# A root of the norm by bits, one Newton step and a third-order step, on rows that one product with ones brings to all partitions

## The chip, the cores and the metric

One core of one Trainium2 chip runs the whole program. The metric is the device time of one execution in microseconds (us). A span, as the trace gives it, is some 2 us shorter than the time. The words TensorE, VectorE, ScalarE, GpSimd stand for the engines that the profile calls PE (PEld for its weight loads), DVE, ACT, POOL.

## The reference

```python
# attention: batch 8, heads 8, sequence 576, head size 64 (retention with decay)
x = attention_output          # 4608 tokens x 512
rms = np.sqrt(np.mean(x * x, axis=-1, keepdims=True) + 1e-06)
xn = x / rms * rms_g
g = xn @ w_gate               # 512 x 1536
silu = g * (1.0 / (1.0 + np.exp(-g)))
val = xn @ w_val
return (silu * val @ w_out).astype(np.float32)
```

Everything is fp32. The tokens are worked in 12 units of 384. Channels lie on partitions (4 blocks of 128), tokens along the free axis. So the mean of squares is a sum over partitions, and its root is wanted on every partition, because each channel of a token is multiplied by the same number.

## The kernel before

The norm of unit u+1 is worked while TensorE does the last product of unit u, a down projection in seven products of 12 matmuls (xo, zo, wo, yo, xo, zo, wo).

```python
def norm_1(u):                       # mean of squares, one column per 128 tokens
    ms = bank(f"ms_{u}")
    for s in range(NS):              # NS = 3
        nc.tensor.matmul(ms[:, s : s + 1], lhsT=t_of[u][:, s * P : s * P + P], rhs=mean_w, ...)
    r = tmp.tile([P, NS], F32, ...)
    nc.vector.tensor_scalar(out=r, in0=ms[:, :NS], scalar1=EPS, scalar2=None, op0=ALU.add)
    nc.gpsimd.tensor_tensor(out=r, in0=r, in1=mhalf.to_broadcast([P, NS]), op=ALU.pow)
    t_of[u] = r

def diagonals(u):                    # three diagonal matrices of the roots
    for s in range(NS):
        nc.vector.tensor_scalar(out=t_of[u][:, s * P : s * P + P], in0=ident,
                                scalar1=r[:, s : s + 1], scalar2=None, op0=ALU.mult)

def norm_2(u):                       # ones times diagonal: the roots as rows on all partitions
    rb = bank(f"rb_{u}")
    nc.tensor.matmul(rb[:, :U], lhsT=ones, rhs=t_of[u], start=True, stop=True)
    for c in range(NHP):             # NHP = 4
        nc.vector.scalar_tensor_tensor(out=x[:, c], in0=x[:, c], scalar=rms_g[:, c : c + 1],
                                       in1=rb[:, :U], op0=ALU.mult, op1=ALU.mult)
    # ... four differences of blocks of x, for the seven-product form of the up projection

# in the loop over units, between the products of across(u):
    # behind xo, zo, wo: norm_1(u + 1), diagonals(u + 1)
    # behind yo, xo:     norm_2(u + 1)
```

`norm_0` before this squares x on ScalarE and adds the four blocks up on VectorE.

Of the kernel before, what the change touches and what calls it, by code (L numbers as in the profile page):

```python
# [10 lines left out]
F32 = mybir.dt.float32  # L11
U32 = mybir.dt.uint32
AF = mybir.ActivationFunctionType
ALU = mybir.AluOpType
P = 128
# [26 lines left out]
def kernel(  # L42
# [11 lines left out]
    nc = tc.nc  # L54
    B, H, S, D = q.shape
    NTOK, DM = out.shape
    DFF = moe_w_gate.shape[1]
    NHP = H // 2
# [5 lines left out]
    U = 384  # L64
    HU = U // 2
    NS = U // P
    NU = NTOK // U
    NH = NF // 2
    NG = NH // 2
    EPS = 1e-6  # L70
    assert (D, DM, NHP * P) == (64, H * D, DM) and S % SQ == 0 and NTOK % U == 0
    assert NC * L == S and NC == 2 * NFULL + 1 and TAIL == L == D and NHP == 4 and NH % 2 == 0
    assert (2 * S) % U == 0 and B % 2 == 0 and S == 3 * HU

    const = ctx.enter_context(tc.tile_pool(name="const", bufs=1))
# [11 lines left out]
    def bank(name):  # L87
        return banks.tile([P, 512], F32, tag="b", name=name)

    def temp(name):  # L90
        return tmp.tile([P, U], F32, tag="t", name=name)

    def cell(name, value):
        t = const.tile([P, 1], F32, name=name)
        nc.vector.memset(t, value)
        return t

    ones = const.tile([P, P], F32, name="ones")
# [10 lines left out]
    gc = const.tile([P, NHP], F32, name="gc")  # L109
    tick = const.tile([1, 1], F32, name="tick")  # L110
    rms_g = const.tile([P, NHP], F32, name="rms_g")
    w_out = const.tile([P, NF, DM], F32, name="w_out")


# [14 lines left out]
    x_of, t_of, h_of, first_places = {}, {}, {}, {}  # L129
# [3 lines left out]
    def load_qk(j):  # L133
        b, hp = jobs[j]
        for nm, src in (("q", q), ("k", k)):

            t = raw.tile([P, S // SQ, SQ], F32, tag=nm + "raw", name=f"{nm}raw_{j}")
            for e in range(2):
                rows = src[b, 2 * hp + e].rearrange("(t b) (i a) -> i b t a", b=SQ, a=SQ)
                for i in range(D // SQ):  # L140
                    r = e * D + i * SQ
                    nc.sync.dma_start(out=t[r : r + SQ], in_=rows[i])
            st[j][nm + "raw"] = t
# [56 lines left out]
    def load_kv(j):  # L200

        b, hp = jobs[j]
        for nm, src, bufs in (("k", k, 4), ("v", v, 3)):
            t = raw.tile([P, NFULL, 2, D], F32, tag=nm, name=f"{nm}_{j}", bufs=bufs)
            for e in range(2):
                nc.sync.dma_start(
                    out=t[:, :, e],
                    in_=src[b, 2 * hp + e, : NFULL * P].rearrange("(c p) d -> p c d", p=P),
                )
            st[j][nm] = t  # L210
        t = st[j]["vt"] = raw.tile([L, 2, D], F32, tag="vt", name=f"vt_{j}", bufs=3)
        nc.sync.dma_start(
            out=t, in_=v[b, 2 * hp : 2 * hp + 2, NFULL * P :].rearrange("e p d -> p e d")
        )
# [182 lines left out]
    def slot(j, rest=True):  # L397

        if j > len(jobs):
            return  # L400
        if rest and j > 0:
            values(j - 1)
        if j < len(jobs):
            scores(j)
            states(j)
        if j < len(jobs):
            weigh(j)
        if j < 2 * NHP:
            sums(j)
        if rest and j > 0:  # L410
            carried(j - 1)
        if 2 * NHP <= j < len(jobs):
            sums(j)

    def prepare_next(j):
        if j + 1 < len(jobs):
            prepare(j + 1)

    def load_next(j):
        if j + 2 < len(jobs):  # L420
            load_qk(j + 2)
            load_kv(j + 2)
# [11 lines left out]

    def gather(u, c, sq):

        if c:
            nc.vector.tensor_tensor(out=t_of[u], in0=t_of[u], in1=sq, op=ALU.add)
        else:
            t_of[u] = sq  # L440

    def norm_0(u):
        for c in range(NHP):
            gather(u, c, square(u, c))

    def norm_1(u):
# [7 lines left out]
        r = tmp.tile([P, NS], F32, tag="r", name=f"r_{u}", bufs=1)  # L454
        nc.vector.tensor_scalar(out=r, in0=ms[:, :NS], scalar1=EPS, scalar2=None, op0=ALU.add)
        nc.gpsimd.tensor_tensor(out=r, in0=r, in1=mhalf.to_broadcast([P, NS]), op=ALU.pow)
        t_of[u] = r

    def diagonals(u):
        r = t_of[u]  # L460
        t_of[u] = temp(f"diag_{u}")
        for s in range(NS):
            nc.vector.tensor_scalar(
                out=t_of[u][:, s * P : s * P + P], in0=ident, scalar1=r[:, s : s + 1],
                scalar2=None, op0=ALU.mult,
            )

    def norm_2(u):



        x = x_of[u]
        rb = bank(f"rb_{u}")
        nc.tensor.matmul(rb[:, :U], lhsT=ones, rhs=t_of[u], start=True, stop=True)
        for c in range(NHP):
            nc.vector.scalar_tensor_tensor(  # L476
                out=x[:, c], in0=x[:, c], scalar=rms_g[:, c : c + 1], in1=rb[:, :U],
                op0=ALU.mult, op1=ALU.mult,
            )
        if u < 2:  # L480
            return
        b11, b12 = x[:, :2, :HU], x[:, :2, HU:]
        b21, b22 = x[:, 2:, :HU], x[:, 2:, HU:]
        t = ffn.tile([P, 3, 2, HU], F32, tag="sums", name=f"sums_{u}")
        t2, t3, t4 = (t[:, i] for i in range(3))
        for o, a, b in ((t3, b22, b12), (b12, b12, b11), (t2, b22, b12), (t4, b21, t2)):
            nc.vector.tensor_tensor(out=o, in0=a, in1=b, op=ALU.subtract)

        t_of[u] = b11, b21, b12, t4, t2, t3, b22
# [116 lines left out]
    def fetch():  # L606
        nonlocal n_fetched
        if n_fetched < 7 * (NU - 2):
            nc.sync.dma_start(
                out=w_slots[:, n_fetched % 4], in_=w_blocks[ORDER[n_fetched % 7]]  # L610
            )
            n_fetched += 1
# [233 lines left out]
    def start():  # L846
# [32 lines left out]
        for j in range(2 * NHP):  # L879
            slot(j)  # L880
            if j + 1 < 2 * NHP:
                turn(j + 1)
            if squares:
                gather(*squares.pop())
            for i in ((1,), (2,), (3,), (4, 5), (6,), (7,), (), ())[j]:
                scale_v(i)
            if j:
                u, c = divmod(j - 1, NHP)
                squares.append((u, c, square(u, c)))
            act(1)  # L890
            if j == 5:
                norm_1(0)
            elif j == 6:
                norm_2(0)
            weights((2, 0, 0, 1, 1, 1, 1, 0)[j])
            if j == 4:
                gather(*squares.pop())
            elif j == 5:
                diagonals(0)
            act(1)  # L900
# [33 lines left out]
        for i, _ in enumerate(rest):  # L934
            if i == 1:
                norm_0(2)
            elif i == 3:
                norm_1(2)
                diagonals(2)
# [5 lines left out]
        for i, _ in enumerate(rest):  # L945
            if i == 2:
                norm_2(2)
# [10 lines left out]
    def behind(u, i):  # L958
        at, n = SLOTS[u % 3]
        if i in at:  # L960
            j = u // 3 * 8 + n + at.index(i)
            slot(j)
            turns.append(j)
            if i < 2 * NG - 1:
                load_next(j)
        if u + 1 < NU and i >= 5:
            (norm_0, norm_1, norm_2)[i - 5](u + 1)
            if i == 6:
                diagonals(u + 1)

    with tc.manual_schedule():
        start()
        for u in range(2, NU):
            for i in range(2 * NG):
                for n, _ in enumerate(up(u, i % 2, i // 2)):
                    if n == 2 and turns:
                        prepare_next(turns.pop())
                if i in (1, 3):
                    fetch()
                    fetch()  # L980
                if i == 2 * NG - 1:
                    rest = across(u)
                    next(rest)
                behind(u, i)
            for i, _ in enumerate(rest):
                if i == 0 and turns:
                    prepare_next(turns.pop())
                if i == 2:
                    behind(u, 6)
                    at, n = SLOTS[u % 3]  # L990
                    if 2 * NG - 1 in at:
                        load_next(u // 3 * 8 + n + len(at) - 1)
                elif i == 4:
                    behind(u, 7)

# [26 lines left out]
```

## Time and profile before

| | before |
|---|---|
| time, median of the first three runs | 1151.86 us |
| time, median with three more runs | 1151.6 us |
| span of the trace (its run took 1153.15 us) | 1151.4 us |
| TensorE / weight loads busy | 98% / 91% |
| VectorE / ScalarE / GpSimd busy | 62% / 21% / 4% |

A row of the timeline reads: start and duration in us, engine, line of the kernel, operation, output<-inputs, and how many instructions were merged. The bracket gives the idle time of the engine before it and what ended that idle time. TensorE executes each fp32 matmul as two instructions, so a product of 12 matmuls shows as x24. The duration of a TensorE row is modelled, so costs are taken from one start to the next. The prediction below shows the rows themselves: TensorE has no idle time around the norm, VectorE has several holes.

### The profile page before, as it was taken

How to read it: one execution, taken by the hardware profiler on the slowest of the kernel's cores; microseconds unless marked ns; L12 is line 12 of the kernel's file. 1: busy time of each engine (PE TensorE's matmuls, PEld its weight loads, DVE VectorE, ACT ScalarE, POOL GpSimd, SP SyncE). 2: the span in 40 equal slices, each digit the busy share in tenths (PEclk: the TensorE clock that was granted, in tenths of full speed). 3: DMA queues.
4: the chain of work that ended last, by engine and by line, in shares of the span. 5: the costliest groups of instructions: out<-in, count | busy, mean ns of one | idle time of the engine just before them, and what ended most of it. 6: DMA issues, size and time to landing. Idle time of an engine off the chain costs nothing.

```text
span 1151.4 us, 24802 instructions
## 1 busy us (share of the span) xinstructions
PE 1126.5 (98%) x10524; PEld 1053.4 (91%) x10524; DVE 716.0 (62%) x1420; ACT 244.0 (21%) x480; POOL 50.8 (4%) x74
## 2 busy tenths in 40 slices
PE   8799999989999999999999999999999999999998
PEld 6655557989999999999999999999999999999998
DVE  5788858675675675365766675465576566445352
ACT  5546542002201211211221120120220220120210
POOL 0000000570000000000000000000000000000000
PEclk8999999999999999999999999999999999999999
DMA  8764336335453565044345456306436503403304
GB/s 203 207 184 147 109 131 193 56 59 117 115 130 67 146 141 160 1 105 102 97 119 73 116 144 119 114 29 120 117 80 140 144 19 93 128 1 99 122 1 110
DMA packets 292943, 125.42 MB, mean 109 GB/s; under 512 B 270432, under 2 KB 275808, under 8 KB 292832
## 3 DMA queue, kind: packets, MB, share of 16 engines
q1 hardware_dynamic: 282688, 107.66, 38.1%
q10 hardware_dynamic: 10144, 16.16, 4.3%
q8 instruction: 83, 1.36, 0.5%
q14 instruction: 28, 0.23, 0.1%
HBM read 108.83 MB, written 14.94 MB: 108 GB/s over the span
## 4 chain that ended last, share of the span: by engine, by line
PE 90%; DVE 3%; DMA 2%; POOL 1%; ACT 1%; issue 1%; SPq 0%; DVEq 0%; POOLq 0%; ACTq 0%
PE x L507 14%; PE w L507 14%; PE z L507 13%; PE up L564 8%; PE xo L629 8%; PE wo L629 7%; PE zo L629 7%; PE y L507 7%; PE yo L629 4%; PE av L351 2%; PE av L370 2%; PE s L280 2%; POOL w_gate L811 1%; PE s L300 1%; DMA w_gate<-in_moe_w_out_dram 1%
## 5 line engine op out<-in xcount | busy, mean ns | idle before, releaser
L531 ACT COPY m<-x 128x384 f32<-128x384 f32 x60 | 28.8, 479 | 449.8 <-PE x L507 425.5
L629 PE MATMUL xo<-h,w_out 128*128 128x192 f32 x528 | 90.3, 328 | 0.0
L507 PE MATMUL w<-sums,w_val 128*128 128x192 f32 x480 | 88.6, 328 | 0.6 <-DVE c L514 0.3
L507 PE MATMUL x<-x,w_gate 128*128 128x192 f32 x480 | 89.0, 329 | 0.0
L507 PE MATMUL x<-x,w_val 128*128 128x192 f32 x480 | 88.8, 328 | 0.0
L507 PE MATMUL z<-x,w_gate 128*128 128x192 f32 x480 | 87.8, 326 | 0.0
L507 PE MATMUL w<-sums,w_gate 128*128 128x192 f32 x480 | 87.8, 326 | 0.0
L507 PE MATMUL z<-x,w_val 128*128 128x192 f32 x480 | 87.8, 326 | 0.0
L629 PEld LDWEIGHTS xo<-h,w_out 128*128 128x128 f32 x528 | 85.9, 190 | 0.6
L629 PE MATMUL wo<-h,w_out 128*128 128x192 f32 x504 | 85.3, 326 | 0.0
L629 PEld LDWEIGHTS wo<-h,w_out 128*128 128x128 f32 x504 | 82.5, 190 | 0.0
L514 DVE TENSOR_TENSOR u<-m,y 128x384 f32<-128x384 f32 x60 | 33.1, 552 | 79.2 <-PE y L507 79.1
L507 PEld LDWEIGHTS w<-sums,w_val 128*128 128x128 f32 x480 | 79.2, 190 | 2.9 <-DVE c L514 2.9
L507 PEld LDWEIGHTS x<-x,w_gate 128*128 128x128 f32 x480 | 79.6, 191 | 0.5
L507 PEld LDWEIGHTS z<-x,w_gate 128*128 128x128 f32 x480 | 79.8, 190 | 0.0
L507 PEld LDWEIGHTS x<-x,w_val 128*128 128x128 f32 x480 | 79.1, 190 | 0.6
L507 PEld LDWEIGHTS z<-x,w_val 128*128 128x128 f32 x480 | 79.6, 190 | 0.0
L507 PEld LDWEIGHTS w<-sums,w_gate 128*128 128x128 f32 x480 | 79.6, 190 | 0.0
L514 DVE TENSOR_TENSOR h<-u,w 128x384 f32<-128x384 f32 x60 | 33.0, 551 | 71.0 <-PE w L507 71.0
L526 ACT ACTIVATE h<-h 128x384 f32<-128x384 f32 x90 | 47.1, 523 | 88.6 <-DVE h L514 88.6
L564 PE MATMUL up<-x,w_gate 128*128 128x384 f32 x192 | 63.3, 488 | 0.9 <-DVE x L476 0.7
L564 PE MATMUL up<-x,w_val 128*128 128x384 f32 x192 | 62.7, 487 | 0.2 <-ACT w_val L572 0.2
(170 smaller groups left out, 1769.8 us busy)
## 6 DMA issues: line engine op xcount, KB each, us to landing
w_out<-w_blocks SPq DMA_DIRECT2D x70, 768.0 KB, 5.1
out_dram<-o SPq DMA_DIRECT2D x368, 24.0 KB, 1.6
qraw<-in_q_dram SPq DMA_DIRECT2D x96, 72.0 KB, 2.7
kraw<-in_k_dram SPq DMA_DIRECT2D x96, 72.0 KB, 2.8
k<-in_k_dram SPq DMA_DIRECT2D x48, 128.0 KB, 3.0
v<-in_v_dram SPq DMA_DIRECT2D x48, 128.0 KB, 2.9
w_out<-in_moe_w_gate_dram ACTq DMA_DIRECT2D x5, 1024.0 KB, 5.8
w_out<-in_moe_w_out_dram ACTq DMA_DIRECT2D x3, 1024.0 KB, 4.9
```

Source lines behind the costliest of these rows:

```text
L280: nc.tensor.matmul(s[side(odd), e, i * L : i * L + L], lhsT=d["kT"][side(e), c * L : c * L + L], rhs=d["qT"][side(e), c * L : c * L + L], ...
L300: nc.tensor.matmul(o[side(e)], lhsT=d["k"][side(odd), i, e], rhs=d["v"][side(odd), i, e], start=True, stop=True,)
L351: mm = nc.tensor.matmul(av[odd][column(j, odd, e), i * L : i * L + L], lhsT=d["v"][side(odd), i, e] if c < NC - 1 else d["vt"][:, e], rhs= ...
L370: mm = nc.tensor.matmul(av[odd][column(j, odd, e), i * L : i * L + L], lhsT=d["sum"][side(e), c - 1], rhs=d["qT"][side(e), c * L : c * L + L],
L507: nc.tensor.matmul(ps[:, i * HU : i * HU + HU], lhsT=w_up[m][:, 2 * blk + c, cut], rhs=t_of[u][blk][:, c], start=(start and i == c == 0), ...
L514: nc.vector.tensor_tensor(out=o, in0=a, in1=pairs_of(ps), op=ALU.add)
L526: nc.scalar.activation(out=o, in_=c, func=AF.Silu)
L531: nc.scalar.copy(out=s1, in_=pairs_of(x_))
L564: nc.tensor.matmul(ps[:, :U], lhsT=w_up[m][:, 4 * half + c, i * P : i * P + P], rhs=x_of[u][:, c], start=(c == 0), stop=(c == NHP - 1),)
L629: nc.tensor.matmul(ps[:, i * HU : i * HU + HU], lhsT=a[:, c, i * P : i * P + P], rhs=rhs[:, c], start=(start and i == c == 0), stop=False, ...
L811: nc.gpsimd.tensor_tensor(out=o, in0=a, in1=b, op=op)
```

## The change

The intent: leave the detour by columns. The squares are summed over partitions by one product with ones, whose result stands on all partitions as rows at once. The inverse root is then computed on 128x384 elements: a first guess out of the bits of the number, one Newton step and one third-order step. This is done for units 3 to 11; the first three keep the old way. (In parts of the diff that are not printed here, EPS moves into the last addition of the squares, and constants are folded into the weights of the norm.)

```diff
+    rms_k = const.tile([P, NHP], F32, name="rms_k")
+    guess = cell("guess", 0x5F1FFFF9 + 2.0**22 * np.log2(DM))
...
+    def root_1(u):
+        y = t_of[u]
+        s = bank(f"ms_{u}")[:, :U]
+        nc.tensor.matmul(s, lhsT=ones, rhs=y, start=True, stop=True)
+        e = temp(f"e_{u}")
+        nc.scalar.activation(
+            out=y.bitcast(U32), in_=s.bitcast(U32), func=AF.Relu, bias=guess, scale=-0.5
+        )
+        nc.scalar.activation(out=e, in_=y, func=AF.Square)
+        nc.vector.scalar_tensor_tensor(
+            out=e, in0=e, scalar=-1.0 / DM, in1=s, op0=ALU.mult, op1=ALU.mult
+        )
+        nc.vector.scalar_tensor_tensor(
+            out=y, in0=e, scalar=K0, in1=y, op0=ALU.add, op1=ALU.mult
+        )
+        nc.scalar.activation(out=e, in_=y, func=AF.Square)
+        t_of[u] = y, e, s
+
+    def root_2(u):
+        y, e, s = t_of[u]
+        nc.vector.scalar_tensor_tensor(
+            out=e, in0=e, scalar=K1 * K1 / DM, in1=s, op0=ALU.mult, op1=ALU.mult
+        )
+        nc.vector.scalar_tensor_tensor(
+            out=e, in0=e, scalar=-10.0 / 3.0, in1=e, op0=ALU.add, op1=ALU.mult
+        )
+        nc.vector.scalar_tensor_tensor(
+            out=s, in0=e, scalar=5.0, in1=y, op0=ALU.add, op1=ALU.mult
+        )
+        t_of[u] = s
...
     def norm_2(u):
-        rb = bank(f"rb_{u}")
-        nc.tensor.matmul(rb[:, :U], lhsT=ones, rhs=t_of[u], start=True, stop=True)
+        g = rms_k
+        rb = t_of[u]
+        if u < 3:
+            g = rms_g
+            rb = bank(f"rb_{u}")[:, :U]
+            nc.tensor.matmul(rb, lhsT=ones, rhs=t_of[u], start=True, stop=True)
...
-            (norm_0, norm_1, norm_2)[i - 5](u + 1)
-            if i == 6:
-                diagonals(u + 1)
+            (norm_0, root_1, norm_2)[i - 5](u + 1)
...
+                elif i == 3 and u + 1 < NU:
+                    root_2(u + 1)
```

More of the change, by code (lines that the diff above doesn't have):

```diff
@@ L70 @@
     EPS = 1e-6
+    K0, K1 = 2.38924456, 0.703952253
     assert (D, DM, NHP * P) == (64, H * D, DM) and S % SQ == 0 and NTOK % U == 0
@@ L435, in gather @@
     def gather(u, c, sq):
-        if c:
+        if c == NHP - 1 and u > 2:
+            nc.vector.scalar_tensor_tensor(
+                out=t_of[u], in0=t_of[u], scalar=EPS * DM / P, in1=sq, op0=ALU.add, op1=ALU.add
+            )
+        elif c:
             nc.vector.tensor_tensor(out=t_of[u], in0=t_of[u], in1=sq, op=ALU.add)
@@ L457, in norm_1 @@
         t_of[u] = r
+    def root_1(u):
[23 more added lines that the diff above has]
+        )
+        nc.vector.scalar_tensor_tensor(
+            out=s, in0=e, scalar=5.0, in1=y, op0=ALU.add, op1=ALU.mult
+        )
+        t_of[u] = s
     def diagonals(u):
@@ L472, in norm_2 @@
         x = x_of[u]
-        rb = bank(f"rb_{u}")
-        nc.tensor.matmul(rb[:, :U], lhsT=ones, rhs=t_of[u], start=True, stop=True)
+        g = rms_k
[4 more added lines that the diff above has]
+            nc.tensor.matmul(rb, lhsT=ones, rhs=t_of[u], start=True, stop=True)
         for c in range(NHP):
             nc.vector.scalar_tensor_tensor(
-                out=x[:, c], in0=x[:, c], scalar=rms_g[:, c : c + 1], in1=rb[:, :U],
+                out=x[:, c], in0=x[:, c], scalar=g[:, c : c + 1], in1=rb,
                 op0=ALU.mult, op1=ALU.mult,
@@ L966, in behind @@
         if u + 1 < NU and i >= 5:
-            (norm_0, norm_1, norm_2)[i - 5](u + 1)
-            if i == 6:
-                diagonals(u + 1)
+            (norm_0, root_1, norm_2)[i - 5](u + 1)
     with tc.manual_schedule():
         start()
+        nc.vector.tensor_scalar(
+            out=rms_k, in0=rms_g, scalar1=3.0 / 8.0 * K1, scalar2=None, op0=ALU.mult
+        )
         for u in range(2, NU):
```

## The prediction

> **What bounds the kernel now.** I read the engine table of the page first, then the chain that ended last, then the list of what TensorE waited for, and last the timeline of one place where the changed lines run.
>
> ```profile
> PE 1126.5 (98%) x10524; PEld 1053.4 (91%) x10524; DVE 716.0 (62%) x1420; ACT 244.0 (21%) x480; POOL 50.8 (4%) x74
> PE 90%; DVE 3%; DMA 2%; POOL 1%; ACT 1%; issue 1%; SPq 0%; DVEq 0%; POOLq 0%; ACTq 0%
> ```
>
> TensorE is busy for 98% of the span and weight loads for 91%; VectorE for 62%, ScalarE 21%, GpSimd 4%. The chain that ended last is TensorE for 90%. The table by stretches says more: from 300 us on, every full 100 us holds 99.65 to 100.00 us of TensorE work, at a granted clock of 1.00. The non-TensorE parts of the chain lie before 250 us, in the start. So in the steady part time can be gained only by taking work out of TensorE's stream, and lost only if something makes TensorE wait.
>
> The norm of each 384-token unit u+1 is worked in the shadow of unit u's last product (the seven-product form of the down projection: products xo, zo, wo, yo, xo, zo, wo). The timeline around 330 us shows the norm of the fourth unit, the first that changes:
>
> ```profile
> 326.07 4.06 PE L629 MATMUL wo<-h,w_out 128*128 128x192 f32 x24
> 326.61 1.35 DVE L641 TENSOR_TENSOR h<-h 128x1152 f32<-128x1152 f32 x1
> 327.88 0.77 DVE L251 STREAM_TRANSPOSE qT<-qraw 128x576 f32<-128x576 f32 x1
> 328.57 0.73 DVE L251 STREAM_TRANSPOSE kT<-kraw 128x576 f32<-128x576 f32 x1
> ...
> 329.97 0.72 PE L450 MATMUL ms<-mean_w,sq 128*128 128x1 f32 x6
> ...
> 330.55 4.15 PE L629 MATMUL yo<-h,w_out 128*128 128x192 f32 x24
> 330.73 0.16 DVE L455 TENSOR_SCALAR r<-ms 128x3 f32<-128x3 f32 x1 [1.43 <-PE ms L450]
> 330.97 0.86 POOL L456 TENSOR_TENSOR r<-r,mhalf 128x3 f32<-128x3 f32 x1 [14.04 <-DVE r L455]
> 331.87 0.68 DVE L463 TENSOR_SCALAR diag<-ident,r 128x128 f32<-128x128 f32 x3 [0.98 <-POOL r L456]
> ...
> 334.54 4.06 PE L629 MATMUL xo<-h,w_out 128*128 128x192 f32 x24
> 334.81 0.56 DVE L638 TENSOR_TENSOR u2o<-m1o,yo 128x384 f32<-128x384 f32 x1 [2.26 <-PE yo L629]
> ...
> 338.44 0.81 PE L474 MATMUL rb<-diag,ones 128*128 128x384 f32 x2
> 338.64 0.58 DVE L651 STREAM_TRANSPOSE o<-xo 128x384 f32<-128x384 f32 x1 [1.49 <-PE xo L629]
> ...
> 339.08 4.06 PE L629 MATMUL zo<-h,w_out 128*128 128x192 f32 x24
> 339.14 1.32 DVE L641 TENSOR_TENSOR h<-h 128x1152 f32<-128x1152 f32 x1
> 340.38 2.18 DVE L476 SCALAR_TENSOR_TENSOR x<-x,rms_g,rb 128x384 f32<-128x384 f32 x4
> ```
>
> The reader is to see three things. The TensorE rows follow each other without an idle bracket, so ms and rb are paid in full. VectorE, in contrast, has holes: 1.43 us before r, 0.98 us before diag, 2.26 us before u2o, 1.49 us before the xo transpose. And GpSimd's power works on 128x3 elements in 0.86 us that nobody on TensorE waits for. The next such places (424, 510, 601 us and so on) repeat these figures within some hundredths.
>
> **What the Trainium skill says.** "TensorE: Matmul & The Clock Gate", section LDWEIGHTS, gives a weight load as columns / 1.2 ns, 107 ns for 128 columns. The six one-column ms matmuls therefore should be bound by their six loads; the trace shows 0.72 us for six, 120 ns each, so it agrees roughly. "VectorE: DVE Perf Modes", section The TRN2 errata, gives (N+151)/0.96 ns for an fp32 tensor_tensor, 557 ns for N=384; the trace has 551 to 558. "ScalarE: Activation LUTs", section What ACT_TABLE_LOAD costs, gives 186 + 0.833 N ns with immediates, 506 ns for 384, and about 93 ns more for a [128,1] bias; the trace's Square has 522. Its section Table sets says cheap functions such as relu are in every set. The trace agrees so far: there is one table load in all, though Silu, Square, Copy and Relu all run, so the new Relu should bring no load.
>
> **The change part by part**, for the nine norms of units 3 to 11 (places at 330, 424, 510, 601, 695, 781, 871, 964 and 1047 us).
>
> TensorE. From wo's first matmul (326.07) to xo's (334.54) are 8.47 us. A 24-matmul product alone takes 342.98 - 339.08 = 3.90 us (the next wo starts at 342.98 in the same timeline), so ms costs 8.47 - 7.80 = 0.67 us. In the same way rb costs 339.08 - 334.54 - 3.90 = 0.64 us. The change puts one product with ones on 384 columns at the place of ms: the shape of rb, so 0.64 us; and it drops rb. Net per norm: 0.64 - 0.67 - 0.64 = -0.67 us. Nine norms: -6.0 us. In instructions: each norm loses six ms and two rb matmuls and gains two, so TensorE should have 10524 - 54 = 10470.
>
> VectorE. Removed per norm: r 0.16 and three diag at 0.283, 1.0 us. Added: five scalar_tensor_tensor on 128x384; the existing one of that size takes 0.606, so 3.0 us; and the last gather becomes one too (0.61 for 0.555). Sum +2.1 us a norm, +19 us over nine: 716 becomes about 735, 64%. ScalarE gains three activations, the first with a pointer bias from PSUM: about 1.6 us a norm, +15 us. GpSimd loses nine powers at about 0.85, -7.7 us. All of this lies beside TensorE's stream, if it fits the holes.
>
> Does it fit? The order of the built program answers where each piece stands. Two scalar_tensor_tensor replace r and diag before u2o, and three stand between the first output transpose and the xo transpose. First part: the ones product ends near 330.6. Relu, Square, two VectorE steps and a Square form one dependent chain: 0.55 + 0.52 + 0.61 + 0.61 + 0.52 = 2.8 us, and some 0.1 to 0.2 us per handover (r started 0.18 us after yo, behind ms). The VectorE steps end near 333.4, ahead of u2o at 334.8; the last Square ends near 334.1. Second part: the first output transpose ends at 337.15. Three dependent steps at about 0.63 take 1.9 us, to 339.0. The xo transpose then starts some 0.4 us later than its 338.64, and so do h (L641) and the four x multiplies. Against this, TensorE now runs 0.67 us earlier. The deadlines: the last wo product needs h (L641), ready near 340.9, and starts at 342.3, slack 1.4 us. The next unit's first product needs two of the x multiplies, ready near 341.9, and starts at 346.2. Its second needs the sums, ready near 344.7, and starts at 347.5. Nothing becomes a wait of TensorE.
>
> **The rivals.** (1) VectorE takes the place of the wait: the three extra steps push h past the last wo product. For it: this is the tightest deadline, 2.5 us of slack before and about 1.4 after; against it, even 0.3 us more per step fits. If the steps took 1.2 us instead of 0.63, the loss would be about 0.3 us a norm, and the total -3 us: 1149. (2) PSUM: the five banks rotate, and the ones product's bank is now held from 330 to about 342.6 instead of being given up early. For it: TensorE's stream would show it at once. Against it: rb's bank is no longer asked for, and the next unit starts only at 346. Cost if wrong: perhaps 0.5 us a norm, 1150. (3) The gain is all hidden because something other than TensorE bounds the place. Against it: no idle bracket stands at these products before. That would be 1151.9. (4) More gain, from GpSimd no longer sitting in the chain: the carried product waits for a GpSimd tick only 3.7 us in all, three times, 3.1 of it in one wait, and the powers run at other places than the ticks. I expect nothing of it. The added rms_k multiply on 128x4 and the memset cost VectorE well under half a microsecond, off the path.
>
> **How the numbers follow.** 1151.86 - 6.0 = 1145.8 us, -0.52%. The runs of before spread over 0.8 us; some 1 us goes for reordering of weight loads around the ones product and for one run against another. The low end supposes 0.85 us a norm gained; the high end supposes rival 1 or 2 at about half of the gain. Range 1143.8 to 1148.6. No path leads to 2%: TensorE would have to lose 23 us of work, where all ms and rb work of the nine norms together is 11.8 us. Nor to 2% slower: 23 us would be 2.6 us of stall a norm. Within 2% gets 0.97.
>
> **What would show each step right or wrong.** Right: TensorE near 1120 us busy and 10470 matmuls; the place near 330 with one two-matmul product of about 0.64 us and none between xo and zo; no line in TensorE's wait list for the ones product's successors; VectorE near 735, ScalarE near 259, GpSimd near 43 us; the xo transpose some tenths after the end of xo. Wrong: idle time on TensorE before wo (L629) put down to h (L641) on VectorE, or before the next unit's first products put down to x or sums; an idle time before the ones product itself; VectorE steps in the root far from 0.61 us; a second table load on ScalarE.

## The result

The changed kernel took 1147.94 us (median of 6 runs, 1144.03 to 1148.23) against 1151.6 us (median of 6 runs, 1151.2 to 1154.66). The ratio is 0.9955, with a 95% interval of 0.9938 to 0.9973. A ratio here is the mean time of one kernel's fast runs over the mean of the other's of the same rounds, so it is not quite the ratio of the medians quoted. The output was correct in every run.

The engine table of the changed kernel:

```profile
PE 1121.7 (98%) x10470; PEld 1049.0 (92%) x10470; DVE 732.5 (64%) x1431; ACT 259.5 (23%) x507; POOL 42.7 (4%) x65
```

TensorE lost the 54 instructions and 4.8 us, and keeps its 98%. VectorE gained 16.5 us and ScalarE 15.5 us, which cost nothing visible. The timeline of the fourth unit's norm in the changed kernel, to be held against the one in the prediction:

```profile
327.65 4.06 PE L676 MATMUL wo<-h,w_out 128*128 128x192 f32 x24
...
331.55 0.81 PE L472 MATMUL ms<-sq,ones 128*128 128x384 f32 x2
...
332.20 4.06 PE L676 MATMUL yo<-h,w_out 128*128 128x192 f32 x24
332.40 0.58 ACT L474 ACTIVATE sq<-ms,guess 128x384 uint32<-128x384 uint32 x1 [6.68 <-PE ms L472]
...
333.57 0.56 DVE L478 SCALAR_TENSOR_TENSOR e<-e,ms 128x384 f32<-128x384 f32 x1 [2.67 <-ACT e L477]
...
334.75 0.53 ACT L484 ACTIVATE e<-sq 128x384 f32<-128x384 f32 x1 [1.22 <-DVE sq L481]
...
336.10 4.06 PE L676 MATMUL xo<-h,w_out 128*128 128x192 f32 x24
336.30 0.56 DVE L685 TENSOR_TENSOR u2o<-m1o,yo 128x384 f32<-128x384 f32 x1 [1.58 <-PE yo L676]
...
338.57 0.52 DVE L491 SCALAR_TENSOR_TENSOR e<-e,ms 128x384 f32<-128x384 f32 x1
...
340.00 4.06 PE L676 MATMUL zo<-h,w_out 128*128 128x192 f32 x24
340.20 0.58 DVE L698 STREAM_TRANSPOSE o<-xo 128x384 f32<-128x384 f32 x1
340.71 1.32 DVE L688 TENSOR_TENSOR h<-h 128x1152 f32<-128x1152 f32 x1
341.94 2.18 DVE L523 SCALAR_TENSOR_TENSOR x<-x,rms_k,ms 128x384 f32<-128x384 f32 x4
...
343.90 4.06 PE L676 MATMUL wo<-h,w_out 128*128 128x192 f32 x24
```

From wo to xo are 336.10 - 327.65 = 8.45 us (8.47 before), and from xo to zo 3.90 us (4.54 before). That is 0.66 us less per norm. Two things follow from the rest. No TensorE row has an idle bracket. And the hole of 1.49 us before the xo transpose is now filled by the three steps from L491 on, yet the transpose starts 0.20 us after the start of TensorE's next product, as before.

A more exact measure than the total is the distance between the norm products of neighbouring units (start of the first matmul to start of the first matmul, from the timelines). In the steady part it hardly depends on chance:

| us between norm products of units | 3-4 | 4-5 | 5-6 | 6-7 | 7-8 | 8-9 | 9-10 | 10-11 |
|---|---|---|---|---|---|---|---|---|
| before | 94.18 | 85.66 | 90.98 | 93.94 | 85.66 | 90.54 | 93.05 | 83.21 |
| before, second trace | 94.18 | 85.66 | 90.54 | 93.95 | 85.66 | 90.54 | 93.06 | 83.22 |
| changed | 93.28 | 84.99 | 89.87 | 93.28 | 84.98 | 89.88 | 92.38 | 82.54 |
| changed, second trace | 93.28 | 84.99 | 89.87 | 93.28 | 84.98 | 89.88 | 92.38 | 82.54 |

Seven of the eight are shorter by 0.66 to 0.68 us (taking the second trace of before, in which the 0.44 us of one interval were gone), the first by 0.90 us. From the last norm product to the end, before needs 104.21 us and the changed kernel 103.45.

Against that stands the start. The first norm product stands at 329.97 us before and at 331.55 us in the changed kernel, 1.58 us later, though the change has nothing in that stretch but a memset and one small multiply. The sum for the two traces: 1.58 - 6.02 (eight intervals) - 0.76 (tail) = -5.2 us, which is 1146.2 - 1151.4. Without the later start it would have been -6.8.

### The profile page after: what moved, and what is told of

Same layout as the page of the kernel before. It is cut to its first block, busy times and chain, and to the rows that moved or that the text cites. A ratio compares the mean times of both kernels' runs of the same rounds, so it can differ in the third digit from the quotient of the medians.

```text
span 1146.2 us, 24711 instructions
## 1 busy us (share of the span) xinstructions
PE 1121.7 (98%) x10470; PEld 1049.0 (92%) x10470; DVE 732.5 (64%) x1431; ACT 259.5 (23%) x507; POOL 42.7 (4%) x65
## 4 chain that ended last, share of the span: by engine, by line
PE 95%; POOL 1%; issue 1%; DVE 1%; ACT 1%; DMA 1%; SPq 0%; ACTq 0%; DVEq 0%; POOLq 0%
PE x L554 14%; PE w L554 14%; PE z L554 13%; PE up L611 11%; PE xo L676 8%; PE wo L676 8%; PE zo L676 8%; PE y L554 7%; PE yo L676 4%; PE av L355 2%; PE av L374 2%; PE s L284 2%; POOL w_gate L858 1%; PE s L304 1%; PE turn_q L234 1%
```

## The experiments

Twelve runs were made, each with runs of the kernel before on the same chip. All had correct outputs and fast states, but for the single run of before again, whose state is unknown.

| run | median us | before | ratio (95%) | interval 4-5 |
|---|---|---|---|---|
| changed again | 1147.22 | 1152.06 | 0.9959 (0.9941-0.9977) | 84.99 |
| ones product twice | 1151.62 | 1152.06 | 0.9998 (0.9983-1.0014) | 85.64 |
| third unit too | 1145.83 | 1152.06 | 0.9943 (0.9929-0.9958) | 84.99 |
| two bf16 parts | 1143.56 | 1152.06 | 0.9925 (0.991-0.9941) | 84.67 |
| two more steps | 1146.47 | 1150.49 | 0.9958 (0.9941-0.9974) | 84.99 |
| six more steps | 1161.88 | 1150.49 | 1.0093 (1.0071-1.0115) | 86.82 |
| GpSimd multiply in chain | 1145.64 | 1150.49 | 0.9951 (0.9933-0.9969) | 84.98 |
| one bf16 part | 1141.18 | 1150.49 | 0.9921 (0.9899-0.9942) | 84.50 |
| GpSimd power in chain | 1147.87 | 1151.84 | 0.9968 (0.9953-0.9984) | 84.99 |
| third unit, two parts | 1142.74 | 1151.84 | 0.9924 (0.9907-0.994) | 84.67 |
| third unit, one part | 1140.98 | 1151.84 | 0.9909 (0.9892-0.9925) | 84.51 |
| before again (one look) | 1152.26 | 1151.84 | - | 85.66 |

The theory: the time follows TensorE's instruction stream in the steady part, and the root hides in VectorE's holes. Rivals: the shorter chain (no GpSimd) or the freed PSUM bank made the gain; VectorE's added work already costs something; the start was made slower by the change.

### The changed kernel once more

No edit.

> The changed kernel once more, for the scatter. Theory (TensorE work): the stretch between the first and the last of the nine norm products is shorter than before by 0.67 us a unit, 5.4 us over eight intervals; the total is 0.5% below before. The first norm product may lie 1 to 2 us earlier or later by the clock of the first 100 us alone (before 329.97 us, changed 331.55 us). Rival (the start was made slower by the change): the first norm product is again 1.5 us later than before at the same granted clock.

All eight intervals came back to the hundredth. The first norm product stood at 333.48 us, later still. The table by stretches shows where the start scatters. For the first 60 us its columns are: stretch, its length, TensorE busy, weight loads busy, VectorE, ScalarE, GpSimd (each with its number of instructions), granted TensorE clock, DMA share, GB/s. For this run:

```profile
0.00:60.00 60.00, 47.43 (x1130) 40.36 (x1133) 36.14 (x117) 31.75 (x78) 2.95 (x13) 0.86 0.78 196
```

And for the run with the GpSimd multiply, which has the same start, and whose first norm product stood at 326.69 us:

```profile
0.00:60.00 60.00, 49.48 (x1256) 41.66 (x1256) 41.26 (x129) 32.08 (x78) 3.05 (x14) 0.94 0.86 219
```

At a granted clock of 0.86, TensorE had issued 1130 instructions after 60 us; at 0.94 it had issued 1256. Before had 0.91 and its changed partner 0.89. Kernels with identical code in the start had their first norm product anywhere from 326.69 to 333.48 us. Of the eleven traces that keep the old norm in the third unit, the four that stood at 331.55 us or later had issued at most 1234 TensorE instructions after 60 us, all others at least 1249: the scatter arises in these 60 us. That the clock causes it is not shown. The traces at 0.91 alone go from 328.29 to 332.45 us, and the DMA share differs along with the clock (0.78 against 0.86 above).

Nor is it shown that the change has no part in it. The nine traces with the changed kernel's start have a mean of 330.0 us, against 329.97 and 329.43 in the two of before. But in the means the five kernels with the changed steady part (changed, changed again, two more steps, both GpSimd runs) are 3.8 to 5.5 us below before, where the steady part accounts for 6.3 (against the second trace of before). A start that is slower by some 1 us is not excluded.

### The product with ones twice

```diff
         nc.tensor.matmul(s, lhsT=ones, rhs=y, start=True, stop=True)
+        nc.tensor.matmul(s, lhsT=ones, rhs=y, start=True, stop=True)
```

> The product with ones is done twice into the same bank, the result is the same. Theory (TensorE's stream is all that counts): plus 0.65 us a unit, nine units, plus 5.8 us against the changed kernel, so level with before within 0.1%; intervals between norm products back to those of before within 0.1 us. Rival (the shorter chain through GpSimd, or the freed PSUM bank, gave the gain): the gain of 0.5% stays, at most 0.1% of it is lost.

The TensorE rows at that place:

```profile
328.29 0.81 PE L472 MATMUL ms<-sq,ones 128*128 128x384 f32 x2
328.93 0.81 PE L473 MATMUL ms<-sq,ones 128*128 128x384 f32 x2
329.57 4.06 PE L677 MATMUL yo<-h,w_out 128*128 128x192 f32 x24
```

Each product costs 0.64 us from start to start. The whole gain is gone: ratio 0.9998, and the intervals are 93.91, 85.64, 90.52, 93.91, 85.63, 90.52, 93.03, 83.19, within 0.04 us of the second trace of before except the first, which is 0.27 shorter. GpSimd is out of the chain here too, and the banks are those of the changed kernel. So neither of these is the gain: 0.64 us of TensorE work a norm is.

The 0.27 us of the first interval has a line. In both traces of before, and in neither of the changed kernel's, TensorE's list of waits has a product at 366 us waiting for VectorE. From the second trace of before (total us, times, longest):

```profile
PE w L507 <- DVE c L514: 0.3, 1, 0.3
```

It is one event per execution. What in the change makes VectorE earlier there was not tried.

### Two and six more VectorE steps

```diff
             out=s, in0=e, scalar=5.0, in1=y, op0=ALU.add, op1=ALU.mult
         )
+        for _ in range(2):      # 6 in the other
+            nc.vector.scalar_tensor_tensor(
+                out=e, in0=e, scalar=0.0, in1=y, op0=ALU.mult, op1=ALU.add
+            )
```

> Two idle VectorE steps of the root's kind behind its last one (they write over a tile nobody reads again). Theory (the root fits VectorE's holes): in the changed kernel the tightest deadline has 1.87 us left (h is ready at 342.03 us, the last wo product starts at 343.90), two steps take 2 x 0.57 = 1.1 us, so the time is that of the changed kernel, plus 0.0 to 0.3 us, and intervals between norm products stay at 93.28, 84.99 and 89.87 us. Rival (VectorE is on the path, the root already costs): plus 1.1 us a unit, 10 us.

> Six such steps, 3.4 us. Theory: 3.4 - 1.87 = 1.6 us (with the handover 1.7 us) of wait a unit, before the last wo product and nowhere else, put down to h on VectorE; nine units, plus 14 to 16 us against the changed kernel, 1.3%. If the slack is bigger than read (or another deadline binds first) the wait shows at another product and with another size.

Two more steps: the intervals stayed (93.29, 84.99, 89.87), except one that was 0.10 longer, and the ratio of 0.9958 is that of the changed kernel. Six more: every interval grew by 1.81 to 1.84 us. In the list of what TensorE waited for:

```profile
PE wo L680 <- DVE h L692: 14.0, 9, 1.6
```

Nine waits at the product and for the operand that the prediction named as the tightest deadline. The first of them:

```profile
336.98 4.06 PE L680 MATMUL zo<-h,w_out 128*128 128x192 f32 x24
...
342.60 4.17 PE L680 MATMUL wo<-h,w_out 128*128 128x192 f32 x24 [1.56 <-DVE h L692]
...
346.61 1.46 PE L558 MATMUL x<-x,w_gate 128*128 128x192 f32 x8
```

The wait moved the start of wo by 342.60 - 336.98 - 3.90 = 1.72 us; the other 0.11 us of the 1.83 is that wo itself took 346.61 - 342.60 = 4.01 us behind its wait, not 3.90. Six steps took 3.52 us, so from one step's start to the next some 0.585 us: 6 x 0.585 - 1.72 = 1.8 us is the slack that was left, against 1.87 read in the trace and 1.4 predicted. The means of the kernels with six and with two more steps (same chip; the latter stands for the changed kernel) differ by 1161.88 - 1146.41 = 15.5 us, within the 14 to 16 expected. The root is therefore hidden with a margin of about three such steps.

### GpSimd back in the chain

```diff
             out=y.bitcast(U32), in_=s.bitcast(U32), func=AF.Relu, bias=guess, scale=-0.5
         )
+        nc.gpsimd.tensor_tensor(out=y[:, :NS], in0=y[:, :NS], in1=ones[:, :NS], op=ALU.mult)
```

> A GpSimd step (times one, 128x3) put back into the chain of the root, behind the bits. Theory: 0.86 us and two handovers lengthen a chain that has 1.6 us of VectorE idle time before the next step, so nothing: 0.0 plus or minus 0.1 us in each interval between norm products, total as the changed kernel. Rival (part of the gain came from GpSimd leaving the chain): 0.1 us or more a unit of the gain is lost.

The intervals did not move, but the test was weak: the multiply took 0.20 us, not the 0.86 expected, since it is the power that is slow. The chain grew by only 0.34 us (the hole before u2o fell from 1.58 to 1.24). So the same with a power with exponent one (`op=ALU.pow`):

> The earlier GpSimd step (times one) took only 0.20 us and so tested little; here it is a power with exponent one, of the kind that took 0.85 us before. Theory: the chain of the root gets some 1.0 us longer than in the changed kernel, VectorE's idle time before u2o falls from 1.58 to some 0.5 us, and intervals between norm products stay within 0.02 us. Rival (a longer chain costs): 0.1 us or more a unit.

```profile
333.96 0.86 POOL L477 TENSOR_TENSOR sq<-sq,ones 128x3 f32<-128x3 f32 x1 [14.70 <-ACT sq L474]
...
337.20 0.56 DVE L686 TENSOR_TENSOR u2o<-m1o,yo 128x384 f32<-128x384 f32 x1 [0.57 <-PE yo L677]
```

The hole before u2o is 0.57 us, one microsecond smaller, as expected, and the eight intervals are within 0.01 us of the changed kernel's. Taking GpSimd out of the chain gave no part of the gain. (The total, 0.9968, is a little above the changed kernel's; the first norm product stood at 332.45 us, a late start.)

### The third unit too

The edit moves the same calls one unit forward, into the start: `root_1(2)` and `root_2(2)` in place of `norm_1(2)` and `diagonals(2)`, and the conditions `u > 2` and `u < 3` by one.

> The new root one unit earlier, in the start. Theory: before, the ones product of rb in that unit stood in a stretch where the first up product waits for GpSimd's combining of the weights (253 us), so taking it out is hidden: 0 to minus 0.1 us against the changed kernel. Rival (every product taken out of TensorE counts alike): minus 0.67 us, which is at the edge of what five rounds show; the place of the next norm product in the trace tells it.

The steps of the root did not hide there. From the timeline and from the list of what TensorE waited for between 236 and 262 us, in this run:

```profile
229.74 0.54 DVE L491 SCALAR_TENSOR_TENSOR e<-e,ms 128x384 f32<-128x384 f32 x1
230.32 1.05 DVE L494 SCALAR_TENSOR_TENSOR e<-e 128x384 f32<-128x384 f32 x1
231.40 1.51 DVE L497 SCALAR_TENSOR_TENSOR ms<-e,sq 128x384 f32<-128x384 f32 x1
```

```profile
PE zo L676 <- DVE u4o L685: 3.2, 1, 3.2
PE av L374 <- POOL tick L363: 1.8, 1, 1.8
```

GpSimd is combining weights then, and VectorE's last two root steps, which read both operands from SBUF, take 1.05 and 1.51 us in place of 0.56 and 0.57. The first, which reads ms from PSUM, takes 0.54 us (0.52 elsewhere). TensorE's wait for VectorE before zo grows from 0.8 to 3.2 us, and its later wait for GpSimd's tick shrinks from 3.1 to 1.8. From this unit's norm product to the next are 124.47 us, against 125.29 and 125.27 in the two traces of the changed kernel. That looks like the 0.8 us of a gain, and I took it for one in the next expectations. It is none: in eleven traces with the old start this stretch lies between 124.00 and 125.56, by whether the granted clock falls behind the 3.1 us wait. With the clock at 1.00 there (the runs with the ones product twice, with the GpSimd multiply and with six more steps) it is 124.00, 124.18 and 124.50, so the third unit changed is not below it. The ratio of 0.9943 lies inside the interval of the changed kernel. So: no gain shown, in line with the theory, though by a way that I had not expected: taking rb out gave TensorE 0.64 us (wo to yo 3.90 us in place of 4.54), and the slowed root steps on VectorE made it wait longer a little later.

### Fewer TensorE passes for the sum

Two variants ask for the sum with bf16 products. With two parts, the sum of squares is copied to bf16 on ScalarE and the remainder is formed on VectorE:

```diff
+            parts = halves[u] = temp(f"halves_{u}").bitcast(BF16).rearrange("p (i t) -> p i t", i=2)
+            nc.scalar.copy(out=parts[:, 0], in_=t_of[u])
+            nc.vector.tensor_tensor(
+                out=parts[:, 1], in0=t_of[u], in1=parts[:, 0], op=ALU.subtract
+            )
...
-        nc.tensor.matmul(s, lhsT=ones, rhs=y, start=True, stop=True)
+        for i in range(2):
+            nc.tensor.matmul(s, lhsT=ones_h, rhs=halves[u][:, i], start=(i == 0), stop=(i == 1))
```

> The sum of squares is split in two bf16 parts (a copy on ScalarE, a difference on VectorE), and two bf16 products with ones add them up in place of the one fp32 product. Theory: each bf16 product of 384 columns takes 162.5 ns, in place of two passes of 322.5 ns, so 0.33 us instead of 0.65 us a unit: minus 0.32 us a unit, minus 2.9 us against the changed kernel; accurate to about one part in 65,000 before averaging, so the result stays right. Rival: the copy and the difference delay the product (slack about 3 us, needed 1.3 us), TensorE waits before it, and the gain is gone.

With one part, the last addition of the squares writes bf16 directly and there is one product:

> The last gather writes one bf16 row block, one bf16 product with ones adds it up. Theory: 0.16 us in place of 0.65 us a unit, minus 0.48 us a unit and minus 4.3 us against the changed kernel; intervals between norm products 92.8, 84.5 and 89.4 us. The sum of 512 squares is rounded to 8 bits in 128 parts, about 0.1% each and some 0.01% in the mean, so the result should still pass. Rival: at 0.16 us the weight load of the product, not its columns, sets its time, and the gain stops at that of two parts.

The TensorE rows at the place, with one part:

```profile
328.54 0.33 PE L481 MATMUL ms<-halves,ones_h 128*128 128x384 bf16 x1
...
328.70 4.06 PE L685 MATMUL yo<-h,w_out 128*128 128x192 f32 x24
```

The product costs 0.16 us from start to start. The intervals fell by 0.31 to 0.33 us with two parts and by 0.47 to 0.49 with one, as TensorE's time says. Medians were 1143.56 and 1141.18 us. So the weight load did not set the time of the single product, as the rival had it. No wait of TensorE appeared at these products. Both outputs passed the comparison; how much margin the single bf16 part leaves was not reported, so two parts are the safer choice.

### Both together

> The root from the third unit on and the two bf16 parts together. Theory: the two gains lie at different places, so they add: minus 0.32 us for each of nine units and minus 0.8 us in the start, minus 3.7 us against the changed kernel, some minus 9 to minus 10 us (0.8%) against before. Intervals between norm products as with two parts alone (92.96, 84.67, 89.55 us). The wait for GpSimd's tick at 253 us is again below 2 us (1.78 us with the third unit alone, 3.1 us without) and the clock in the 7 us behind it stays at 1.00. If the clock falls below 0.9 there all the same, the shorter wait is not what kept it up.

> The same with one bf16 part. Theory: minus 0.48 us for each of nine units and minus 0.8 us in the start, minus 5.1 us against the changed kernel, some minus 10 to minus 11 us (0.9%) against before; intervals 92.80, 84.50 and 89.39 us. The wait for the tick at 253 us as in the other.

1142.74 us (ratio 0.9924) and 1140.98 us (0.9909): below the changed kernel by about what the bf16 parts alone give. Against before, the medians are lower by 9.1 and 10.9 us, within what was expected; but 0.8 us of that expectation was the gain that is none, so this agreement is luck. Nothing of the third unit shows beyond its scatter. Its stretch was 124.74 and 123.81 us. The wait for the tick was below 1 us and the clock behind it 1.00, as expected, but TensorE's wait of 3.2 us before zo was there instead, and the clock in the stretch from 240 to 253 us was 0.82 and 0.91: the stall had moved, not gone. In the run with one part one interval (6-7) was 0.22 us longer than with one part alone; its cause was not looked into.

The fastest version tried is thus one bf16 part, with or without the third unit: about 0.8 to 0.9% below before, in place of the change's 0.45%.

### Before once more

> The kernel before once more, for one question: in its first trace two intervals between norm products (94.18 and 90.98 us) are 0.27 and 0.46 us longer than in the run with the ones product done twice (93.91 and 90.52), the other six within 0.03 us. If these are chance of one execution, they come back to 93.9 and 90.5 here, and the change is worth 0.65 us a unit and not more. If they belong to the kernel (a stall that the change removes), they stay.

Of the two odd intervals, one came back to the common figure (90.54 in place of 90.98), the other stayed at 94.18. So 0.44 us of the first pair of traces was chance, and 0.27 us belongs to the kernel before, as its wait list says. This is one execution, so its total of 1152.26 us says little.

## Why the prediction was right

- **The bound.** It named TensorE's stream in the steady part. Right: doing the one product twice takes the whole gain away (0.9998), and making it cheaper adds to it, each by TensorE's time.
- **The size a norm.** It had 0.67 us. The intervals show 0.66 to 0.68. Beside this came one event of 0.27 us that it had not seen. TensorE's 10470 instructions were exact.
- **VectorE's holes.** It had the steps end before u2o and the tightest deadline at the last wo product. Right: with six more steps exactly that product waits for exactly that operand. The sizes were off: it took 0.606 us a step from a row whose instruction has a scalar per partition. The new steps with an immediate took 0.52 to 0.57. So VectorE rose by 16.5 and not 19 us, the xo transpose was not 0.4 us later at all, and the slack was 1.8 and not 1.4.
- **ScalarE and GpSimd.** 259.5 and 42.7 us, against 259 and 43. No table load was added.
- **Rivals.** VectorE, the banks, a hidden gain and GpSimd were each argued against and left out of the estimate; the runs agree for all four. The high end of the range, though, was room for the first two.
- **The total.** 1145.8 was said and 1147.94 measured, inside the range, but 2.1 us high and near its upper end. That end supposed a rival that did not come true, so that the total still fell inside is in part luck. The step that was mis-sized is the 1 us allowed for "one run against another". The first norm product alone scatters by 6.8 us for identical code. The six runs of the changed kernel span 4.2 us, and eleven of before 6.6 us. The three runs known at prediction time, 0.8 us apart, gave too good a picture. Whether the change also slows the start by some 1 us stays open. Where that scatter is looked away from, in the steady part, the predicted 6.0 us became 6.02 + 0.76 = 6.8, of which 0.7 are the two events (0.44 and 0.27 us) in that trace of before.

## What to carry to other kernels

Where one engine's rows follow each other without idle brackets, a change is worth what it takes out of that stream, start to start, and other engines may even do more, up to the slack of the tightest deadline; read this slack off the trace, then test it by adding steps until the wait appears. Distances between the same instruction of neighbouring iterations can show 0.02 us where totals scatter by several. And the same code moved to a place with other neighbours (here GpSimd at work, a later wait that ends last) need not bring the same gain.

## What the Trainium skill lacked or had wrong

- "TensorE: Matmul & The Clock Gate", section Back-to-back issue gap, gives a matmul's pace as columns / 2.4 + 2.5 ns. No page gives a time for fp32 (how many passes it takes stands elsewhere in the skill). In these traces an fp32 matmul is two instructions of about twice that time each: 162.5 ns for 192 columns, 0.64 us for a whole product of 384. For bf16 the formula held: 0.16 us for 384 columns.
- The same page, section LDWEIGHTS, gives 107 ns for 128 columns and has no figure for fp32. The bf16 load took 0.10 us; fp32 loads are shown with 190 ns, and six in a row (the old ms) took 0.67 us of TensorE's stream, 0.11 us each (the prediction's 120 ns divides their modelled duration).
- The same page, section What's actually happening, puts the fall of the clock after an idle window of about 3.4 us. Here a wait of 3.1 us was followed by a granted clock below 1 in eight of eleven traces (0.70 and 0.80 in the two stretches behind it in before) and not in three. It calls the ramp at the start less than 1% of a kernel and variable. Here the first norm product of identical code differed by 6.8 us of 1150, 0.6%, which is more than the change was worth; that this is the ramp is not shown.
- "VectorE: DVE Perf Modes", section The TRN2 errata, has a measured formula for tensor_tensor and a general row of cycles, but nothing measured for scalar_tensor_tensor. One on 128x384 took 0.606 us with a scalar per partition and 0.52 to 0.57 us with an immediate.
- "GPSIMD Engine Reference" has no figure for the power: on 128x3 elements it took 0.85 us, a multiply 0.20 us.
- "Perfetto Trace Analysis", section Optimizing Scalar/DVE Operations, says that GpSimd and VectorE share a read port; that sentence gives no size. Beside GpSimd's elementwise work the two root steps with both operands in SBUF took 1.05 and 1.51 us in place of 0.56 and 0.57; the one with an operand in PSUM took 0.54 (0.52 elsewhere).
